# Two row tiles turned by transfer instead of on TensorE, and two gradient rows computed earlier

## The chip, the cores and the metric

The kernel runs on one core of a Trainium2 chip. A core has five engines that run side by side and wait for each other through semaphores: TensorE (PE, matrix products), VectorE (DVE), ScalarE (ACT), GpSimd (POOL) and SyncE (SP). SP's main work here is to issue transfers (DMAs), which 16 transfer engines carry out. An engine works through its instructions in the order that was fixed when the kernel was built; so does the queue of transfers that SP issues. The metric is device time in microseconds (us), lower is better.

## The reference

The reference computes one block and all its gradients. `xn` is the layer norm of the input `x` (2048 rows, 1024 columns); the output is `x + A(xn) + B(xn)`, where A is a gated long convolution and B is a gated network. Only B and its backward pass matter for this change:

```
gate = xn @ W_gate                 # 1024 -> 3584
up   = xn @ W_up
h    = relu(gate) * up
out += h @ W_down                  # 3584 -> 1024
# backward, with g the gradient of the output:
gh   = g @ W_down^T
grad_up, grad_gate = gh * relu(gate), gh * (gate > 0) * up
# and from these the gradients of W_gate, W_up, W_down and of x
```

All tensors are bf16; products are summed in f32.

## The kernel before

**Tiles and blocks.** Rows come in 16 tiles of 128, and the 3584 hidden columns in 7 blocks of 512. The first phase, `hidden`, goes over 14 blocks: 7 column blocks for row tiles 0 to 7, then the same 7 for row tiles 8 to 15. For each block and row tile it makes three products with `gemm8` (line 1088), each of 8 matmuls 128x128 by 128x512: the gate into `ps_g`, the up into `ps_u`, and the gradient row (`grad_row`) into `ps_h`. The first two read a turned tile of normalised rows (`xT[s]`, tile `xnT`: the contraction has to lie along the partitions) and the weight tiles `wg` and `wu`. The third reads a turned tile of the gradient (`gT[s]`, tile `goT`) and the turned `W_down` (`wdT`). ACT copies the gate through a ReLU into `ru` (line 1196); DVE masks the up (1203) and makes `ht` (1209), which is stored to `h_d` (1214). After a gradient row, ACT copies `ps_h` to `gh` (1331), DVE multiplies `ru` by it (1332), and `ru` is stored to `ug_d` (1337).

**Where turned tiles come from.** `goT` and `wdT` are read from DRAM by transposing transfers that SP issues (`load_T`, line 1112; `row_piece_T`, 1106). The normalised rows don't exist at the start: the layer norm makes them in the first block, chunk by chunk (`layer_norm`, a generator that is advanced by `next(ln)`; `chunk` takes three steps). DVE scales a tile (line 987), POOL stores it to `xn_d` (990), and in the first block `flip_xn` turns it: 8 PE transposes of 128x128 into a PSUM bank (line 1127, `pst_x`) and one or two copies to `xnT` (1132). For row tiles 8 to 15, in the second half, `xnT` is read back from `xn_d` by transposing transfers.

**Order in the first block** (`n == 0`, `ahead` is true). `first_rows` makes gates and ups of rows 0 to 3. Then the loop over `sp = 0, 2, 4, 6` issues: gradient rows `sp` and `sp + 1` (`grad(sp)`), and gates and ups of rows `sp + 4` and `sp + 5` (`gate_up(sp + 4)`), as long as there are any. So the order is: gradient rows 0, 1; gates and ups 4, 5; gradient rows 2, 3; gates and ups 6, 7; gradient rows 4, 5, 6, 7. Within `grad(0)` tiles 4 and 5 are turned, and within `grad(2)`, after the first matmul of row 3, tiles 6 and 7 (`flip_ahead`).

**Weights of the next block.** At the end of `gate_up(6)` the transfers for the second block are traced: `wg` (`load_gate`), `wu` (`load_up`, line 1081) and the second half of `wdT` (`load_down(2)` and `load_down(3)`). The new `wg` is put where the old one lies, so its first piece waits until gate row 7 has read that piece; so does `wu`, behind the ups. The new `wdT` has a place of its own.

**What sets an engine's order.** The instructions of this stretch have priorities by the order of the code (`pri.now()`), and a scheduler takes on each engine, by its own model of time, the first in priority that is ready. An instruction that waits for nothing, such as the transfers of `goT` and `wdT`, can so be issued ahead of older ones that wait. `tc.issue_after(ins)` keeps the instructions traced under it behind `ins`, if they are on the same engine as `ins`; it has no effect on other engines.

Of the kernel before, what the change touches and what calls it, by code (L numbers as in the profile page):

```python
# [17 lines left out]
P = 128  # L18
# [854 lines left out]
class LnMlp:  # L873
# [246 lines left out]

    def flip_xn(self, st):
        xT = self.act_tile("xnT", st)
        h = self.DT // 2 if st < 3 else self.DT
        for k0 in range(0, self.DT, h):
            pst = self.ps.tile([P, self.DT, P], BF16, name="pst_x", tag="bps")
            for kt in range(k0, k0 + h):
                self.pri.pin(self.nc.tensor.transpose(pst[:, kt, :], self.xn[st][:, kt * P:(kt + 1) * P],  # L1127
                                                      self.ident[:]), always=True)
            c = h // 2 if st == 0 and k0 == 0 else h
            for k in range(k0, k0 + h, c):  # L1130
                copy = self.nc.scalar.copy if st == 4 else self.nc.vector.tensor_copy
                self.copied = copy(out=xT[:, k * P:(k + c) * P], in_=pst[:, k:k + c, :].rearrange("p a b -> p (a b)"))  # L1132
                if st < 5:
                    self.tc.keep_in_program_order(self.copied)
        return xT
# [11 lines left out]
    def hidden(self, first, goT, load, ln, tables, Wg, Wu, Wd, g, xn_d, h_d, ug_d):  # L1147


        nc, HS, N = self.nc, self.ST // 2, 2 * self.FB  # L1150
        w, sets, spare = first, (0, 1, 2), 3
        self.g_nat, self.hs = [None] * self.ST, [None] * (self.ST // 2)
        xT, gT = [], goT
        for n in range(N):
            half, fb = divmod(n, self.FB)
            s0, cols, ahead = half * HS, slice(fb * 512, fb * 512 + 512), n == 0
            swap, last = fb == self.FB - 1, n == N - 1
            if n and fb == 0:
                xT, gT = nxT, ngT
# [8 lines left out]
            def load_gate():  # L1168
                if last:
                    self.slab_part(h_d, 0, "hs", self.hs, 4, sg)  # L1170
                else:
                    nw[0] = self.col_block(Wg, nb, "wg", sg)

            def load_up():
                if not last:
                    nw[1] = self.col_block(Wu, nb, "wu", su)

            def load_down(q):
                if last and q == 0:
                    self.slab_part(h_d, 0, "hs", self.hs, 0, spare)  # L1180
                elif not last:
                    if q == 0:
                        nw[2] = []
                    nw[2].append(self.row_piece_T(Wd, nb, "wdT", spare, q))

            def flip(k):
                while len(xT) < k:
                    while len(self.xn) <= len(xT):
                        next(ln)
                    xT.append(self.flip_xn(len(xT)))  # L1190

            def gate(s, held=False):
                ru[s] = self.e2_tile("ru")
                ps = self.ps_tile("ps_g")
                self.gemm8(ps, xT[s], wg)
                self.pri.pin(nc.scalar.activation(out=ru[s][:, 0, :], in_=ps[:], func=ACT.Relu), always=held)  # L1196

            def up(s, mid=None, after={}, put=lambda *fs: [f() for f in fs], hold=False):
                ps = self.ps_tile("ps_u")
                self.gemm8(ps, xT[s], wu, mid, after)  # L1200

                def masked():
                    return self.pri.pin(nc.vector.scalar_tensor_tensor(  # L1203
                        out=ru[s][:, 1, :], in0=ru[s][:, 0, :], scalar=0.0, in1=ps[:], op0=ALU.is_gt, op1=ALU.mult),
                        always=hold)

                def product():
                    ht = self.e1_tile("ht")
                    self.pri.pin(nc.vector.tensor_tensor(out=ht[:], in0=ru[s][:, 0, :], in1=ru[s][:, 1, :],
                                                         op=ALU.mult), always=hold)  # L1210

                    def store(r=(s0 + s) * P, cols=cols, ht=ht):
                        queue = nc.gpsimd if n == 0 and s < 4 else nc.sync
                        self.stored = queue.dma_start(out=h_d[r:r + P, cols], in_=ht[:])
                        self.pri.pin(self.stored)
                    self.defer(store)
                put(masked, product)

            def step(ns=1730):
                yield ns  # L1220
                self.tick()
# [41 lines left out]
            def gate_up(sp):  # L1263
                end = sp == HS - 2
                if ahead:
                    flip(sp + 2)
                for s in (sp, sp + 1):
                    gate(s)
                    yield from step(self.PACE[0])
                if end:  # L1270
                    load_gate()
                for s in (sp, sp + 1):
                    up(s)
                    yield from step(self.PACE[1])
                if end:
                    load_up()
                    if ahead:
                        for q in range(2, 4):
                            load_down(q)
                if swap:  # L1280
                    next_rows(sp)

            def next_rows(sp):
                for s in (sp, sp + 1):
                    if last:
                        self.g_nat[2 * sp + s - sp] = self.load_nat(g, 2 * sp + s - sp, "g_nat", s)
                    else:
                        nxT.append(self.load_T(xn_d, HS + s, "xnT", s))
# [32 lines left out]
            def flip_ahead(sp):  # L1321
                flip(min(sp + 6, HS))
                if sp == 0:
                    with self.tc.issue_after(self.copied.ins):
                        chunk()

            def grad_row(s, after={}):
                ps = self.ps_tile("ps_h")
                self.gemm8(ps, gT[s], wd, None, after)
                gh = self.e1_tile("gh")  # L1330
                self.pri.pin(nc.scalar.copy(out=gh[:], in_=ps[:]))  # L1331
                self.pri.pin(nc.vector.tensor_tensor(out=ru[s][:], in0=ru[s][:], in1=gh[:].rearrange(
                    "p (o f) -> p o f", o=1).to_broadcast([P, 2, 512]), op=ALU.mult))

                def store(r=(s0 + s) * P, cols=cols, t=ru[s]):
                    queue = nc.gpsimd if n == 0 and s < 2 else nc.sync
                    self.pri.pin(queue.dma_start(out=ug_d[r:r + P, :, cols], in_=t[:]))
                self.defer(store)
                yield 1730
                self.tick()  # L1340
# [8 lines left out]
            def grad(sp):  # L1349
                for s in (sp, sp + 1):  # L1350
                    at = 3 if sp == 0 else 0
                    yield from grad_row(s, {at: lambda: flip_ahead(sp)} if ahead and s == sp + 1 else {})
                if swap:
                    next_grads(sp)

            def chunk(steps=3):
                with self.tc.issue_after(self.ln_act.ins):
                    for _ in range(steps):
                        next(ln)
# [8 lines left out]
            for sp in range(0, HS, 2):  # L1368
                self.pri.now()
                while len(gT) < min(sp + 4, HS):  # L1370
                    gT.append(self.load_T(g, len(gT), "goT", HS + len(gT)))
                if ahead or sp < HS - 4:
                    if not ahead:
                        load_down(sp // 2)
                        yield from gate_up(sp)
                        self.hold = self.busy = False
                    yield from grad(sp)
                elif sp == HS - 4:
                    yield from last_rows(sp)
                if ahead:  # L1380
                    with self.tc.issue_after(self.stored.ins):
                        if sp in (0, 4):
                            load(6 + sp // 4)
                        if sp == 0:
                            for q in range(2):
                                load_down(q)
                if ahead and sp + 4 < HS:
                    yield from gate_up(sp + 4)
                if n == 1 and sp in (0, 2):
                    with self.tc.issue_after(self.stored.ins):  # L1390
                        load(8 + sp // 2)
                if ahead and sp == 4 or n == 1 and sp in (0, 6):
                    chunk()
                if ahead and sp == 4:
                    with self.tc.issue_after(self.ln_act.ins), self.tc.issue_after(self.ln_dve.ins):
                        tables()
# [474 lines left out]
```

## Time and profile before

| what | before |
|---|---|
| time, median of 3 runs | 1856.0 us (1855.65 to 1856.48) |
| profiled execution | 1856.27 us, of which the span from first to last instruction is 1854.5 us |
| granted TensorE clock | 1.000 of full speed |
| DVE, ACT, POOL busy, share of the span | 60%, 35%, 1% |
| chain that ended last | PE 99%, DMA 1% |
| matmul 128x512, mean duration (they overlap) | 379 ns |
| transposes of `xn` on PE (`pst_x`), 64 of them | 219 ns median duration, 7.2 to 38.1 us |
| copies `xnT` from PSUM on DVE | 11, of 0.278 to 0.692 us |
| transposing transfers `goT`, time on SP's queue | 1.259 / 1.427 / 3.837 us (least, median, most) |
| transposing transfers `wdT`, time on SP's queue | 1.246 / 1.344 / 4.083 us |

Times within the profile count from the span's first instruction. "SPq" is the queue on which SP issues transfers; the time shown there is that of issuing, and a transfer lands later. The time of a transposing transfer that stands in the timeline is therefore no time of arrival. The first block is the stretch up to about 53 us, and the whole change lies in it.

### The profile page before, as it was taken

The numbers are of one execution on the slowest core, as the hardware profiler recorded it, in microseconds if no ns is written. First come the engines' busy times: TensorE is split into PE (matmuls) and PEld (weight loads), VectorE is DVE, ScalarE is ACT, GpSimd is POOL, SyncE is SP. The second block draws the span as 40 slices with busy tenths as digits, with TensorE's granted clock in tenths as the row PEclk, the third lists the DMA queues.
The fourth block names the chain that finished last, engine by engine and source line by source line (L and its number), as shares of the span: only waits on it lengthen the run. The fifth ranks groups of instructions, "written<-read, shape, count | busy, mean of one in ns | idle before, by whom it ended". The sixth has DMA issues, their size and how long they took to land.

```text
span 1854.5 us, 32107 instructions
## 1 busy us (share of the span) xinstructions
PE 1846.5 (100%) x13061; PEld 846.8 (46%) x13061; DVE 1115.5 (60%) x1634; ACT 646.5 (35%) x1215; POOL 26.6 (1%) x63
## 2 busy tenths in 40 slices
PE   9999999999999999999999999999999999999999
PEld 4444444444444444444444444444444544444444
DVE  6656797698779769585785667721122222566652
ACT  5644544444444454544544554320000000111100
POOL 1000000000000000000000000000000000000000
PEclk9999999999999999999999999999999999999999
DMA  9897679968766857549566444379999757799963
GB/s 271 240 222 185 155 170 228 233 153 202 171 165 192 257 138 186 129 133 251 155 156 162 138 132 140 125 220 260 246 250 247 181 144 165 177 210 214 207 149 74
DMA packets 746084, 344.64 MB, mean 186 GB/s; under 512 B 575832, under 2 KB 715088, under 8 KB 745936
## 3 DMA queue, kind: packets, MB, share of 16 engines
q1 hardware_dynamic: 732944, 312.96, 70.5%
q10 hardware_dynamic: 9504, 17.04, 2.9%
q0 software_dynamic: 3488, 12.58, 1.9%
q8 instruction: 102, 1.67, 0.4%
q14 instruction: 46, 0.38, 0.1%
HBM read 143.79 MB, written 103.83 MB: 134 GB/s over the span
## 4 chain that ended last, share of the span: by engine, by line
PE 99%; DMA 1%; ACT 0%; DVE 0%; issue 0%; ACTq 0%; DVEq 0%
PE ps_x L1721 21%; PE ps_w L1424 20%; PE ps_h L1088 10%; PE ps_u L1088 10%; PE ps_g L1088 10%; PE ps_o L1589 10%; PE ps_d L1424 9%; PE ps_c L83 4%; PE ps_d L1440 2%; PE ps_w L1440 1%; DMA wu<-in_B_W_up_dram 0%; PE ps_r L1623 0%; DMA ug_d<-ru 0%; DMA ln_x<-in_A_q_dram 0%; PE pst_x L1127 0%; ACT arena L87 0%
## 5 line engine op out<-in xcount | busy, mean ns | idle before, releaser
L1424 PE MATMUL ps_w<-ugs,xn_nat 128*128 128x512 bf16 x1728 | 381.1, 379 | 0.0
L87 ACT CAST arena<-ps_c 128x512 bf16<-128x512 f32 x576 | 293.9, 610 | 84.8 <-PE ps_c L83 84.4
L1088 PEld LDWEIGHTS <-xnT 128*128 128x128 bf16 x1792 | 171.8, 98 | 209.7 <-issue 6.5
L1424 PEld LDWEIGHTS <-xn_nat 128*128 128x128 bf16 x1728 | 165.3, 98 | 201.2 <-issue 6.7
L341 DVE STREAM_TRANSPOSE arena<-arena 128x1024 f32<-128x1024 f32 x96 | 180.3, 1933 | 126.4 <-ACT arena L87 108.5
L1088 PE MATMUL ps_u<-wu,xnT 128*128 128x512 bf16 x896 | 206.0, 379 | 0.6 <-DMA wu<-in_B_W_up_dram 0.6
L1088 PE MATMUL ps_g<-wg,xnT 128*128 128x512 bf16 x896 | 205.1, 379 | 0.4 <-DVE xnT L1132 0.3
L1088 PE MATMUL ps_h<-wdT,goT 128*128 128x512 bf16 x896 | 203.8, 379 | 1.0 <-ACT ru L1196 1.0
L1721 PE MATMUL ps_x<-wgT,ggT 128*128 128x512 bf16 x896 | 198.6, 379 | 0.0
L1721 PE MATMUL ps_x<-wuT,guT 128*128 128x512 bf16 x896 | 198.6, 379 | 0.0
L1739 ACT ACTIVATE w<-xn,m 128x512 f32<-128x512 bf16 x32 | 24.3, 807 | 481.6 <-DVE m L1732 368.2
L1589 PE MATMUL ps_o<-wd,hT 128*128 128x512 bf16 (+1 forms) x896 | 187.6, 372 | 0.0
L1424 PE MATMUL ps_d<-g_nat,hs 128*128 128x512 bf16 x768 | 169.9, 379 | 0.0
L1721 PEld LDWEIGHTS <-guT 128*128 128x128 bf16 x896 | 87.7, 98 | 105.7
L1721 PEld LDWEIGHTS <-ggT 128*128 128x128 bf16 x896 | 87.7, 98 | 105.5
L1088 PEld LDWEIGHTS <-goT 128*128 128x128 bf16 x896 | 86.5, 98 | 105.1 <-issue 2.5
L1589 PEld LDWEIGHTS <-hT 128*128 128x128 bf16 x896 | 87.7, 98 | 99.9
L1331 ACT CAST gh<-ps_h 128x512 bf16<-128x512 f32 x112 | 66.3, 592 | 189.2 <-PE ps_h L1088 177.6
L1427 ACT CAST wi<-ps_w 128x512 bf16<-128x512 f32 x108 | 64.6, 598 | 189.7 <-PE ps_w L1424 155.4
L1203 DVE SCALAR_TENSOR_TENSOR ru<-ru,ps_u 128x512 bf16<-128x512 bf16 x112 | 76.3, 682 | 84.2 <-PE ps_u L1088 46.8
L1581 DVE TENSOR_TENSOR ya<-ya,xe 128x1024 bf16<-128x1024 bf16 x16 | 11.1, 692 | 177.3 <-DMA xe<-xn_d 177.3
L91 DVE TENSOR_TENSOR t<-arena 128x2048 bf16<-128x2048 bf16 x96 | 113.8, 1218 | 0.4
(146 smaller groups left out, 1402.1 us busy)
## 6 DMA issues: line engine op xcount, KB each, us to landing
ugs<-ug_d SPq DMA_DIRECT2D x112, 256.0 KB
ug_d<-ru SPq DMA_DIRECT2D x110, 256.0 KB
wg<-in_B_W_gate_dram SPq DMA_DIRECT2D x56, 256.0 KB
wu<-in_B_W_up_dram SPq DMA_DIRECT2D x56, 256.0 KB
hs<-h_d SPq DMA_DIRECT2D x56, 256.0 KB
out_dram<-wi SPq DMA_DIRECT2D x56, 256.0 KB
h_d<-ht SPq DMA_DIRECT2D x108, 128.0 KB
gt<-in_grad_out_dram SPq DMA_DIRECT2D x32, 256.0 KB
```

The costliest lines, as they stand in the source:

```text
L83: self.pri.pin(self.nc.tensor.matmul(out, lhsT=lhsT, rhs=rhs, start=start, stop=stop))
L87: self.pri.pin(self.nc.scalar.copy(out=out, in_=in_))
L91: self.pri.pin(self.nc.vector.tensor_tensor(out=out, in0=in0, in1=in1, op=op))
L341: self.pri.pin(self.nc.vector.transpose(out=df[:, c0:c0 + 32, :], in_=sf[:, c0:c0 + 32, :]))
L1088: self.pri.pin(self.nc.tensor.matmul(ps[:], lhsT=xT[:, kt * P:(kt + 1) * P], rhs=w(kt), start=(kt == 0), stop=(kt == self.DT - 1)), always ...
L1203: return self.pri.pin(nc.vector.scalar_tensor_tensor(out=ru[s][:, 1, :], in0=ru[s][:, 0, :], scalar=0.0, in1=ps[:], op0=ALU.is_gt, op1=ALU ...
L1331: self.pri.pin(nc.scalar.copy(out=gh[:], in_=ps[:]))
L1424: self.pri.pin(self.nc.tensor.matmul(ps[:], lhsT=lhsT(st), rhs=rhs(st), start=(st == 0), stop=(st == self.ST - 1)))
L1427: self.pri.pin(self.nc.scalar.copy(out=out, in_=ps[:]))
L1440: self.pri.pin(self.nc.tensor.matmul(ps[i][:], lhsT=lhsT(i, st), rhs=rhs(i, st), start=(st == 0), stop=(st == self.ST - 1)))
L1589: nc.tensor.matmul(ps, lhsT=hT[:, kt, :], rhs=self.wd[:, kt, oc], start=(kt == 0), stop=(kt == self.FT - 1))
L1721: nc.tensor.matmul(ps, lhsT=T[:, kt, :], rhs=W[:, kt, oc], start=(i == 0), stop=(i == n - 1))
```

## The change

Three edits. First, `flip_xn` turns tiles 6 and 7 (`st > 5`) by a transposing transfer on SP that reads the normalised tile in on-chip memory (SBUF) and writes `xnT` there, in place of eight PE transposes and a DVE copy for each; the last such transfer is kept as `self.turned`. Second, in the first block two groups of transfers on SP are kept behind `self.turned`: the second half of the next `wdT`, and `goT` 6 and 7. (For `goT` 4 and 5 the edge goes to `self.copied`, a DVE instruction, and has no effect on SP.) Third, `grad(4)` is traced right after `grad(2)`, ahead of `gate_up(6)`; the order of the products in the first block becomes: gradient rows 2, 3, 4, 5; gates and ups 6, 7; gradient rows 6, 7.

```diff
     def flip_xn(self, st):
         xT = self.act_tile("xnT", st)
+        if st > 5:
+            self.turned = self.nc.sync.dma_start_transpose(out=xT[:].rearrange("p (a b) -> p a b", b=P),
+                                                           in_=self.xn[st])
+            return xT
         h = self.DT // 2 if st < 3 else self.DT
...
                 if end:
                     load_up()
                     if ahead:
-                        for q in range(2, 4):
-                            load_down(q)
+                        with self.tc.issue_after(self.turned.ins):
+                            for q in range(2, 4):
+                                load_down(q)
...
             for sp in range(0, HS, 2):
                 self.pri.now()
                 while len(gT) < min(sp + 4, HS):
-                    gT.append(self.load_T(g, len(gT), "goT", HS + len(gT)))
+                    with self.tc.issue_after(self.turned.ins if sp == 4 else self.copied.ins):
+                        gT.append(self.load_T(g, len(gT), "goT", HS + len(gT)))
...
-                    yield from grad(sp)
+                    if not ahead or sp != 4:
+                        yield from grad(sp)
+                    if ahead and sp == 2:
+                        yield from grad(4)
```

## The prediction

> **What bounds the kernel.** I read the page's busy times first, then what TensorE (PE) waits for after 12 us, then the timelines of PE and of SP's queue in the first 60 us, and last the busy share of the transfer engines in that stretch.
>
> ```profile
> PE 1846.5 (100%) x13061; PEld 846.8 (46%) x13061; DVE 1115.5 (60%) x1634; ACT 646.5 (35%) x1215; POOL 26.6 (1%) x63
> ```
>
> PE is busy for 1846.5 of 1854.5 us. What shortens PE's own work shortens the kernel; any new wait of PE lengthens it, for there is almost no wait in which to hide one:
>
> ```profile
> PE ps_h L1088 <- ACT ru L1196: 1.0, 1, 1.0
> PE ps_u L1088 <- DMA wu<-in_B_W_up_dram: 0.6, 1, 0.6
> PE ps_g L1088 <- DVE xnT L1132: 0.3, 1, 0.3
> ```
>
> (In total, times, longest.) From 12 us on PE waits three times, for 1.9 us together, the third of them at the very start. Now PE around the change (start, length, what, count):
>
> ```profile
> 35.74 1.67 PE L1088 MATMUL ps_h<-wdT,goT 128*128 128x512 bf16 x7
> 37.26 1.06 PE L1127 MATMUL pst_x<-ident,ln_x 128*128 128x128 bf16 x16
> 38.15 1.67 PE L1088 MATMUL ps_h<-wdT,goT 128*128 128x512 bf16 x7
> 39.66 3.62 PE L1088 MATMUL ps_g<-wg,xnT 128*128 128x512 bf16 x16
> 43.11 3.62 PE L1088 MATMUL ps_u<-wu,xnT 128*128 128x512 bf16 x16
> 46.57 7.07 PE L1088 MATMUL ps_h<-wdT,goT 128*128 128x512 bf16 x32
> 53.47 3.62 PE L1088 MATMUL ps_g<-wg,xnT 128*128 128x512 bf16 x16
> ```
>
> The 16 transposes of tiles 6 and 7 sit inside gradient row 3; then come gates and ups of rows 6 and 7 (39.66, 43.11), gradient rows 4 to 7 in one run (46.57), and at 53.47 the second block, which needs new weights wg and, from 56.93, wu. The queue that fetches them:
>
> ```profile
> 33.19 3.00 SPq L1112 DMA_TRANSPOSE goT<-in_grad_out_dram  x2
> 36.24 3.02 SPq L1106 DMA_TRANSPOSE wdT<-in_B_W_down_dram  x2
> 39.30 4.02 SPq L1112 DMA_TRANSPOSE goT<-in_grad_out_dram  x2
> 43.44 0.99 SPq L1214 DMA_DIRECT2D h_d<-ht  x2
> 44.52 1.31 SPq L1337 DMA_DIRECT2D ug_d<-ru  x2
> 45.93 2.17 SPq L1081 DMA_DIRECT2D wg<-in_B_W_gate_dram  x4
> ...
> 53.03 1.25 SPq L1337 DMA_DIRECT2D ug_d<-ru  x2
> ```
>
> SP issues without a pause from 33.19 to 51.39, and the transfer engines are full (stretch, length, busy time of each engine; the last three figures are the granted clock, the transfer engines' busy share and GB/s):
>
> ```profile
> 36.20:43.30 7.10, 7.10 (x46) 3.71 (x45) 3.62 (x7) 1.77 (x3) 1.02 (x2) 1.00 1.26 231
> 43.30:48.10 4.80, 4.80 (x24) 2.18 (x23) 2.22 (x4) 0.60 (x1) 0.00 (x0) 1.00 0.92 260
> 48.10:51.40 3.30, 3.30 (x17) 1.53 (x16) 1.25 (x2) 1.77 (x3) 0.00 (x0) 1.00 0.94 273
> ```
>
> Shares of 0.92 to 1.26 mean that whatever is added lands later. When each transfer lands is in the trace's semaphore records (each transfer raises its semaphore in 16 steps; the last one counts); PE's need is the start of the matmul that reads the piece:
>
> ```
> transfer   SP issue      landed   PE needs it   margin
> goT 4, 5   33.19-36.20   37.43, 38.25
> wdT 2, 3   36.24-39.26   41.23, 43.68
> goT 6, 7   39.30-43.33   44.56, 45.48
> ug_d 2, 3  44.52-45.83   47.14, 47.94
> wg 0..3    45.93-48.10   49.51 50.55 52.23 52.97   53.47 53.90 54.34 54.77   3.96 3.35 2.11 1.80
> wu 0..3    48.19-51.39   53.68 54.73 55.45 56.50   56.93 57.36 57.79 58.22   3.25 2.63 2.34 1.72
> ```
>
> The smallest margin, 1.72 us (wu's last piece), carries the forecast.
>
> **Part by part.**
>
> *16 PE transposes go.* The first starts at 37.26, the matmul behind them at 38.15: **0.89 us** of PE time saved (55.6 ns each). Tiles 6 and 7 alone change. Weighed against a rule: the Trainium skill (TensorE: Matmul & The Clock Gate, "Part 4: PE-mode transpose") gives about 275 ns for such a transpose inside a kernel, by which 16 would be 4.4 us, an estimate from that page. Here they follow each other at 55.6 ns in a full pipeline, so the row decides.
>
> *Two DVE copies go* (1.28 us at 38.47). DVE is idle for 3.9 us at 41 to 45; PE waits for no later DVE result here: nothing. If that cover were gone, at most 1.28.
>
> *Gradient rows 4 and 5 move ahead of gates 6 and 7.* The same 16 matmuls, 3.45 us, at another place: nothing for PE. They need goT 4 and 5 at 38.77 and 40.50 instead of 46.57 and 48.30; landed at 37.43 and 38.25, so nothing, with 1.3 us to spare. Behind the late PE instructions gates 6 and 7 start at 39.66 − 0.89 + 3.45 = 42.22 and at 43.95.
>
> *Two SP transposes are added.* They wait for the normalised tiles; DVE scales them at 35.35 to 36.22 and SP is free at 36.2, so SP hardly stands still. In the queue they take the places of wdT 2 and 3, which landed at 41.23 and 43.68; needed 42.22 and 43.95. Just in time, 1.0 and 0.3 us to spare, a little less if the store of h row 4, ready at 35.4, is issued ahead. No row of this trace is a transpose out of on-chip memory. The nearest are the wdT and goT transposes, of the same 256 KB: from below, 0.9 us between landings when nothing disturbs them (43.68, 44.56, 45.48); from above, (45.48 − 38.25)/4 = 1.81, other traffic included. SP itself spends 1.36 to 1.66 us on most of them. I take 1.2 each, between the transfer's 0.9 and SP's 1.5, since both limit here: **2.4 us for the two, 1.8 to 3.6**. A rule that would lower it: the Trainium skill (DMA: Bandwidth & Descriptors, "Why small descriptors are slow (HBM only)" and "Where 436 GB/s comes from") says that on-chip copies don't suffer from small pieces and that 435 GB/s bounds them, transposes included; that makes 0.6 us each, an estimate from that page, and the end 1.2 us earlier than by my value. No run here shows it.
>
> *wdT 2, 3 and goT 6, 7 are queued behind those two.* goT 6 and 7 land some 2.4 us later, at 47 and 48; their rows now start at 42.22 + 6.91 = 49.13 and 50.86. wdT is wanted in the second block at 60.4. Nothing by themselves; but all four still stand ahead of wg, and so the whole queue moves back by the 2.4.
>
> *The stores of rows 4 and 5 (ug_d) overtake the weights.* This is no line of the diff. Rows 4 and 5 now end at 42.22 and their products are ready some 1.5 us after; wg can't be fetched before gate 7 has read the old piece (43.95 + 0.43). So these stores, at 53.03 before, come ahead of wg. ug_d 2 and 3 landed 0.80 us apart: **1.6 us** for two. If they stay behind, nothing.
>
> *The gate of the old weights.* wg comes free at 44.4 to 45.7 instead of 41.8 to 43.1; since SP reaches wg only after 45.93 anyway, this adds nothing to the queue.
>
> *Sum.* wg and wu land 2.4 + 1.6 = 4.0 us later (3.4 to 5.2), and PE wants them 0.89 earlier. wu's last piece: 56.50 + 4.0 = 60.5 against 57.33: PE loses 3.2 in several waits at the second block's start and has gained 0.89. Net: 4.0 − 1.72 = **+2.3 us** (+1.7 to +3.5). Later work has no wait to absorb that. The profiled execution took 1856.27 us (span 1854.5 and 1.8 around it), 0.27 over the median of 1856.0: it becomes 1858.6, the median **1858.3**.
>
> **Rivals.**
>
> 1. *All hidden* (1855.1). The new transposes fill a hole: between 42.1 and 43.7 transfers lay still here (wdT 3 and goT 6 land 0.9 after that), and if the stores stay behind wg and the hole takes most of the two transposes, the shift stays under 1.72 − 0.89 = 0.8 us. Then only −0.89 is left. For it: the hole is in the record. Against: SP needs 1.36 us for each issue in any case, and the stores are ready too early. In between, stores behind and transposes at 1.2, lies 2.4 − 1.72 = +0.7, 1856.7.
>
> 2. *Slower outright* (1861.9). Transposes out of on-chip memory run at the worst pace of this stretch, 2.98 us (38.25 to 41.23): 6.0 + 1.6 − 1.72 = +5.9. Gate 6 would then wait too, but that wait lies ahead of the same late weights and is not added. It is over 0.2% from 1.9 + a little us per transpose on: (3.7 + 1.72 − 1.6)/2 = 1.9. For it: no row shows such a transpose, and these already swing between 0.9 and 3. Against: packet size and count would be alike.
>
> 3. *A larger gain*: the 16 transposes cost their shown duration, 219 ns each, 3.5 us, with nothing late: 1852.5; and the rule above would give 1851.6. The pitch of 55.6 ns speaks against it.
>
> 4. *The change doesn't do what it says*: the transposes are issued behind other stores, and PE waits at 42.22 for about as long as it saved: 1856.0 to 1857.
>
> **Numbers.** Forecast (+1.7 to +3.5): 0.46. Stores behind (about +0.7): 0.12. All hidden: 0.20. Slower outright (over +3.5): 0.15. Larger gain: 0.02. Not as said: 0.05. Two in ten left out, most of them in the slow tail and the large gain: 1855.0 to 1860.4. A measurement of this kernel tells about 0.2% (3.7 us) from no change. Below 1852.3 lies only rival 3 in its larger form, 0.02; above 1859.7 rival 2 and a little of the forecast's upper end, 0.15; the rest, 0.83, is within.
>
> **What would show it.** PE's timeline: no pst_x at 37, row 3 in one run, rows 4 and 5 at 38.8, gate 6 at 42.2 without a wait. SP's timeline: goT 4, 5, two xnT, wdT 2, 3, goT 6, 7, then stores of four rows ahead of wg. PE's waits: DMA wg and DMA wu at the second block's start, about 3 us in all; with none of these, rival 1 holds. Gates 6 and 7 waiting for xnT by over 1 us, or two xnT landing more than 1.9 us apart, is rival 2. The forecast is wrong if wg is issued before the stores of rows 4 and 5, or if the queue reaches wg less than 2.5 us later than at 45.93.

## The result and the profile after

The kernel after takes **1863.04 us** in the median of 7 runs (1861.35 to 1870.74), the kernel before 1856.07 us in 7 runs beside it (1855.65 to 1856.48): ratio 1.0041 (over all runs; the two medians alone give 1.0038), 95% interval 1.0031 to 1.0051. The forecast was 1858.3 us (1855.0 to 1860.4). The direction was right, and so was the first part of the mechanism, weights that come late at the second block's start; what follows from these waits was missing, and the size was not right. The profiled execution took 1863.04 us with a span of 1861.3 us, 6.8 more than before's.

Busy times of the page, and what PE waits for from 12 us on (in total, times, longest):

```profile
PE 1835.6 (99%) x12833; PEld 846.5 (45%) x13045; DVE 1115.1 (60%) x1632; ACT 644.6 (35%) x1213; POOL 26.6 (1%) x63
```
```profile
PE ps_g L1088 <- DMA wg<-in_B_W_gate_dram: 2.6, 3, 1.1
...
PE ps_h L1088 <- ACT ru L1200: 2.4, 1, 2.4
...
PE ps_h L1088 <- DMA goT<-in_grad_out_dram: 1.0, 2, 0.7
```

PE's busy time is no measure here, since 212 matmul records are missing (12833 against 13045 weight loads). The waits tell more: those for `wg` are the forecast ones; `goT` is new, and the one for ACT's `ru` has grown from 1.0 to 2.4 us. PE around the change:

```profile
35.58 7.07 PE L1088 MATMUL ps_h<-wdT,goT 128*128 128x512 bf16 x31
42.49 3.62 PE L1088 MATMUL ps_g<-wg,xnT 128*128 128x512 bf16 x16
45.94 3.62 PE L1088 MATMUL ps_u<-wu,xnT 128*128 128x512 bf16 x16
49.95 3.79 PE L1088 MATMUL ps_h<-wdT,goT 128*128 128x512 bf16 x15 [0.39 <-DMA goT<-in_grad_out_dram]
54.62 1.30 PE L1088 MATMUL ps_g<-wg,xnT 128*128 128x512 bf16 x4 [0.89 <-DMA wg<-in_B_W_gate_dram]
56.49 0.59 PE L1088 MATMUL ps_g<-wg,xnT 128*128 128x512 bf16 x2 [0.57 <-DMA wg<-in_B_W_gate_dram]
58.20 4.00 PE L1088 MATMUL ps_g<-wg,xnT 128*128 128x512 bf16 x10 [1.12 <-DMA wg<-in_B_W_gate_dram]
```

Gradient rows 2 to 5 run as one group, without the transposes, and gate 6 starts at 42.49 without a wait (forecast 42.22). Then each piece of `wg` lets PE do two matmuls and wait again. The queue on SP that brings them:

```profile
36.53 0.52 SPq L1218 DMA_DIRECT2D h_d<-ht  x1
37.15 4.02 SPq L1124 DMA_TRANSPOSE xnT<-ln_x  x2
41.26 0.53 SPq L1218 DMA_DIRECT2D h_d<-ht  x1
41.84 1.23 SPq L1106 DMA_TRANSPOSE wdT<-in_B_W_down_dram  x1
43.17 0.68 SPq L1342 DMA_DIRECT2D ug_d<-ru  x1
43.90 2.38 SPq L1106 DMA_TRANSPOSE wdT<-in_B_W_down_dram  x1
46.32 1.30 SPq L1112 DMA_TRANSPOSE goT<-in_grad_out_dram  x1
47.73 0.56 SPq L1342 DMA_DIRECT2D ug_d<-ru  x1
48.33 1.38 SPq L1112 DMA_TRANSPOSE goT<-in_grad_out_dram  x1
49.81 1.21 SPq L1342 DMA_DIRECT2D ug_d<-ru  x2
51.11 2.21 SPq L1081 DMA_DIRECT2D wg<-in_B_W_gate_dram  x4
```

`wg` is issued at 51.11 instead of 45.93: 5.18 later. It landed at 54.58, 55.29, 56.45 and 58.16, which is 4.2 to 5.2 later. Last, stretches of 1 us (length, busy time of PE, PEld, DVE, ACT and POOL, then the granted clock, the transfer engines' share and GB/s):

```profile
57.00:58.00 1.00, 0.08 (x1) 0.00 (x0) 0.97 (x7) 0.00 (x0) 0.18 (x2) 1.00 1.01 322
58.00:59.00 1.00, 0.80 (x3) 0.32 (x3) 1.00 (x3) 0.00 (x0) 0.00 (x0) 0.66 1.03 384
59.00:60.00 1.00, 1.00 (x4) 0.36 (x3) 0.48 (x1) 0.82 (x2) 0.00 (x0) 0.50 1.10 412
60.00:61.00 1.00, 1.00 (x3) 0.29 (x2) 0.00 (x0) 1.00 (x1) 0.00 (x0) 0.50 1.03 379
61.00:62.00 1.00, 1.00 (x4) 0.39 (x3) 0.55 (x2) 0.41 (x2) 0.15 (x1) 0.63 1.07 396
62.00:63.00 1.00, 1.00 (x6) 0.48 (x5) 0.25 (x1) 0.76 (x2) 0.00 (x0) 1.00 1.05 389
```

The granted clock falls to half at 58.32 for 3.41 us, and PE's weight loads follow each other at 0.43 us instead of 0.216, though now its data is there.

Every execution has its mean granted clock on record. One fall of 3.41 us lowers the mean of 1861 us by 0.0009, so 0.999 tells of one such fall and 0.998 of two. (The clock falls also behind PE's last matmul; in the profiled spans that lasts at most 1.3 us, too little for the third digit.) Two of the seven executions have 1.000 and took 1861.35 and 1862.31 us; three have 0.999 and took 1862.71 to 1863.57; two have 0.998 and took 1863.92 and 1870.74. So the clock is only a part of the loss: without a fall 5 to 6 us are left.

**Where the 6.8 us lie.** I matched PE's weight loads of both traces one by one and took the lag of after (a start in after less that of the same load in before):

```
at 50 us (gain -0.89, lag from before row 2 +0.27, goT 6 +0.55)     -0.06
waits for goT 7 and the four pieces of wg, 50 to 58.2 us            +3.49
clock at half, 58.3 to 61.7 us                                      +1.69
132 to 144 us                                                       +0.68
278 us (a wait for wu of before is gone)                            -0.78
353 to 359 us (ACT's ru, behind a store of ug_d)                    +1.36
end                                                                 +0.43
sum                                                                 +6.81
```

The wait at 353 to 359 us on ACT's side:

```profile
358.87 0.60 ACT L1200 ACTIVATE ru<-ps_g 128x512 bf16<-128x512 f32 x1 [5.42 <-DMA ug_d<-ru]
```

### The profile page after: what moved, and what is told of

The parts are those of the page before. It is cut to its first block, busy times and chain, and to the rows that moved or that the text cites. A ratio compares the mean times of both kernels' runs of the same rounds, so it can differ in the third digit from the quotient of the medians.

```text
span 1861.3 us, 31864 instructions
## 1 busy us (share of the span) xinstructions
PE 1835.6 (99%) x12833; PEld 846.5 (45%) x13045; DVE 1115.1 (60%) x1632; ACT 644.6 (35%) x1213; POOL 26.6 (1%) x63
## 4 chain that ended last, share of the span: by engine, by line
PE 94%; DMA 2%; SPq 1%; issue 1%; DVE 0%; ACT 0%; ACTq 0%; DVEq 0%
PE ps_x L1730 21%; PE ps_w L1433 20%; PE ps_o L1598 10%; PE ps_h L1088 10%; PE ps_u L1088 9%; PE ps_g L1088 9%; PE ps_d L1433 9%; PE ps_c L83 4%; PE ps_d L1449 1%; SPq L1106 1%; PE ps_w L1449 1%; DMA goT<-in_grad_out_dram 1%; DMA wg<-in_B_W_gate_dram 1%; DMA wu<-in_B_W_up_dram 0%; DMA ugs<-ug_d 0%
## 5 line engine op out<-in xcount | busy, mean ns | idle before, releaser
L1433 PE MATMUL ps_w<-ugs,xn_nat 128*128 128x512 bf16 x1675 | 375.7, 379 | 4.4 <-issue 2.4
```

The source lines that it names most:

```text
L1433: self.pri.pin(self.nc.tensor.matmul(ps[:], lhsT=lhsT(st), rhs=rhs(st), start=(st == 0), stop=(st == self.ST - 1)))
```

## The experiments

The theory after this result: the bytes that now stand ahead of `wg` make it late, and the idle time that follows trips the clock. The rivals were the order of the products, the transposes' kind of memory, the place in SP's queue, and a cost of the late part of the kernel. Times are medians, with the range and number of runs; ratios are to the kernel before on the same chip, where its median was 1856.0 to 1857.1 us, and are worked out over all runs, so they are not quite the quotients of the medians. Each edit is to the kernel that is named.

**e1: the order alone** (before, with the third edit of the change; PE still turns all tiles).

```diff
-                    yield from grad(sp)
+                    if not ahead or sp != 4:
+                        yield from grad(sp)
+                    if ahead and sp == 2:
+                        yield from grad(4)
```


> Only the order of the products is changed; tiles 6 and 7 are turned on PE as before. Theory Q (the weights wg and wu land late because two transposing transfers, 4.0 us of SP's time, and the stores of gradient rows 4 and 5, 1.2 us, come ahead of them; the waits then halve the clock for 3.4 us): only the 1.2 of the stores is left, wg lands 1.2 to 1.6 us later than before, which is under its margin of 1.8 us, so PE waits 0 to 0.3 us and the time is before + 0 to 0.5 (1856.0 to 1856.6). Rival O (the order alone is at fault, since the old weights come free 2.6 us later): waits of 2 us and more at the second block's start, 1858 or more.

1856.8 us (1855.5 to 1860.4, 11), ratio 1.0006 (0.9997 to 1.0014). The stores go as forecast, four together and ahead of `wg` (SP's queue):

```profile
44.88 2.68 SPq L1337 DMA_DIRECT2D ug_d<-ru  x4
47.65 2.27 SPq L1081 DMA_DIRECT2D wg<-in_B_W_gate_dram  x4
```

`wg`'s last piece lands at 54.25, 1.28 later than before, which the margin of 1.80 takes: no wait. The order alone costs nothing that these runs can tell (the interval would still hold 2.6 us).

**e2: the transfers alone** (after without the third edit: `grad(4)` stays where it was).

```diff
-                    if not ahead or sp != 4:
-                        yield from grad(sp)
-                    if ahead and sp == 2:
-                        yield from grad(4)
+                    yield from grad(sp)
```

> Only the two transposing transfers; gradient rows 4 and 5 stay behind gates and ups 6 and 7. Gate 6 is then due at 38.8 us and tile 6 lands at about 42.2: PE waits 3.4 us there. Theory Q: net 3.4 - 0.9 = +2.5 if the clock holds and about +4.2 if a wait of 3.4 us halves it for 3.4 us; wg is 4 us late but so is PE, so no wait of more than 0.5 us at the second block's start (1858.5 to 1860.3). Rival O: this version without the new order is near before, 1855 to 1857.

1869.02 us (1865.44 to 1872.71, 5), ratio 1.0070 (1.0058 to 1.0083): slower than the whole change, and far above the 1858.5 to 1860.3 expected, which counted one long wait and at most one fall of the clock.

```profile
PE ps_g L1088 <- DMA xnT<-ln_x: 4.1, 1, 4.1
PE ps_h L1088 <- DMA goT<-in_grad_out_dram: 3.6, 2, 3.5
```

Gate 6 is now wanted 3.5 us earlier and waits 4.1 us for its tile; the scheduler also put `goT` 7 behind `wu`, so that PE waits again. The clock falls to half for 3.41 us with each of the two waits. So the third edit, taken together with the transfers, saves more than it costs by bringing two stores ahead of `wg`: it is what buys the transposed tiles their time.

**e3: the clock by itself** (after, with 14 matmuls that nobody reads at the end of the first block).

```diff
             self.hold = self.busy
+            if ahead:
+                ps = self.ps_tile("ps_fill")
+                for _ in range(14):
+                    self.pri.pin(nc.tensor.matmul(ps[:], lhsT=xT[0][:, 0:P], rhs=gT[0][:, 0:512], start=True,
+                                                  stop=True), always=True)
```


> The changed kernel with 14 matmuls (3.0 us) added at the end of the first block, whose result nobody reads; they fill the time in which PE waits for wg. Theory Q with the clock: the clock stays at 1.00 in the second block, and although PE has 3.0 us more work the time falls by 1.3 to 1.7 us, to 1861.3 to 1861.8. Rival C (the clock's drop at 58.3 us has nothing to do with the waits): the clock drops all the same and the time stays at 1863 or rises.

1861.30 us (1860.18 to 1863.06, 7), ratio 1.0028 (1.0016 to 1.0039): 1.74 us *faster* than after (by the medians of two sets of runs, beside which before took 1856.01 and 1856.07), with 14 matmuls (3.0 us at 0.216) more work. They fill the time in which PE waited for `wg`. The granted clock is 1.000 in all seven executions; in stretches of 2 us around the place:

```profile
56.00:58.00 2.00, 2.00 (x11) 0.88 (x9) 1.43 (x11) 0.88 (x1) 1.99 (x5) 1.00 1.04 309
58.00:60.00 2.00, 2.00 (x11) 0.90 (x10) 1.97 (x9) 0.61 (x2) 0.69 (x3) 1.00 1.02 358
```

So 1.7 us of the loss is the clock, and it answers to PE standing idle, not to what it waits for.

**e4 and e5: one group each out from ahead of `wg`.** e4 is after with the stores of gradient rows 4 and 5 behind `wu`, e5 is after with `wdT` 2 and 3 behind `wu` (`self.loaded`, new in both, is the last transfer of the weights).

```diff
e4
-                self.defer(store)
+                if n == 0 and s in (4, 5):
+                    self.kept.append(store)
+                else:
+                    self.defer(store)
...
+                if ahead and sp == 2:
+                    with self.tc.issue_after(self.loaded.ins):
+                        for f in self.kept:
+                            f()
e5
-                        with self.tc.issue_after(self.turned.ins):
+                        with self.tc.issue_after(self.loaded.ins):
                             for q in range(2, 4):
                                 load_down(q)
```


> The changed kernel, but the two stores of gradient rows 4 and 5 are issued on SP behind wu. Theory Q: wg lands 1.2 us earlier than in the changed kernel, the waits for it fall from 3.3 to about 2.1 us, net 1.2 us less, 1861.8; if the shorter waits spare the clock, another 1.7 less, 1860.1. If the stores' place does not matter (transfers limited elsewhere): 1863.0.

> The changed kernel, but the second half of the next wdT (two transposing transfers, 1.7 us of SP each) is issued on SP behind wu instead of ahead of wg. Theory Q: SP reaches wg about 3.5 us earlier than in the changed kernel, that is 1.5 us later than before, within the margin of 1.8 us; no wait for wg, none for goT 6, the clock stays, and what is left is PE's saving: before - 0.9 to before (1855.1 to 1856.0). Rival W (wdT itself is then late: it lands at 58 to 60 us and row 0 of the second block reads its third piece at 60.3): PE waits up to 2 us there, 1856 to 1858.

e5: 1858.88 us (1856.34 to 1863.02, 11), ratio 1.0013 (1.0004 to 1.0022); 1.1 us of waits for `wg` and 1.2 for `wu` are left where none was expected, and the clock holds in the profiled execution; `wdT` makes PE wait in neither e5 nor e6, so the rival there is out. e4: 1863.84 us (1859.91 to 1865.18, 5), ratio 1.0036 (1.0023 to 1.0049), no gain in the median. In its profiled execution the second block's start did what was expected (0.7 us for `wg`, 1.1 for `wu`, full clock), but the place at 353 us, far from the change, got worse:

```profile
353.22 1.90 PE L1089 MATMUL ps_u<-wu,xnT 128*128 128x512 bf16 x8
358.65 3.57 PE L1089 MATMUL ps_h<-wdT,goT 128*128 128x512 bf16 x8 [3.53 <-ACT ru L1202]
```

PE waits 3.5 us for a `ru` of ACT, and the clock is at half for 6.83 us (the eight matmuls of 358.65 take 3.57 us instead of 1.9): about 5.4 us more than before at this place alone. The clock divides the five executions of e4: two at 1.000 took 1859.91 and 1859.96 us, which is what was expected with the clock spared; three at 0.999 or 0.998 took 1863.84 to 1865.18.

**e6: both together** (e4 and e5).

> As the run before, and the stores of gradient rows 4 and 5 also behind wu and wdT. Theory Q: wg lands about 0.3 us later than before; no waits at the second block's start, before - 0.9 to before - 0.5 (1855.1 to 1855.5). Rival W: the same late wdT as in the run before, and the stores, now later still, may hold up ru in the second block: 1856 to 1858.

1858.8 us (1856.26 to 1861.43, 11), ratio 1.0012 (1.0003 to 1.0020). PE's waits in its profiled execution of 1856.26 us:

```profile
PE ps_h L1089 <- ACT ru L1202: 0.9, 1, 0.9
PE ps_h L1089 <- DVE ru L1209: 0.7, 1, 0.7
```

No wait at the second block's start is left, the clock holds, and at 50 us PE is 1.24 us ahead of before; at 144 us this lead is gone (0.27 behind). The easing is worth 4.2 us of the 7.0, but the median stays 2.4 above before's 1856.4. Here, too, the clock divides the executions: five at 1.000 took 1856.26 to 1857.95 us, six at 0.999 took 1858.80 to 1861.43.

**e7 and e8: what two more transposes cost, and whether their source matters.** Both are before, plus two transposed transfers of 256 KB into memory that nobody reads; PE still turns all tiles. In e7 the source is the normalised tile on chip, in e8 the gradient in DRAM.

```diff
e7
+        if st > 5:
+            t = self.ln_x[3][:, st - 4, :]
+            self.nc.sync.dma_start_transpose(out=t.rearrange("p (a b) -> p a b", b=P), in_=self.xn[st])
e8
+        if st > 5:
+            t = self.ln_x[3][:, st - 4, :]
+            self.nc.sync.dma_start_transpose(out=t.rearrange("p (a b) -> p a b", b=P), in_=self.g_rows[st * P:(st + 1) * P, :])
...
+        self.g_rows = g
```


> The kernel before (PE transposes, old order), with two transposing transfers of the normalised tiles 6 and 7 added on SP ahead of wg, into memory that nobody reads. Theory Q: SP reaches wg 3.3 to 4 us later; PE's need is unchanged, margins 1.72 to 1.8, so waits of 1.5 to 2.3 us at the second block's start, net the same (1857.5 to 1858.3), up to 1860 if the clock drops. Rival S (a transfer that reads on-chip memory is dearer than one that reads DRAM): over 1 us worse than the run after this one.

> The same with the two added transfers reading the gradient's rows in DRAM. Theory Q: a transposing transfer costs SP about 1.7 us whichever memory it reads, so the same delay of wg and the same time as the run before this one within 1 us (1857.5 to 1858.3). Rival S: 1 us or more faster than that run.

e7: 1858.61 us (1856.25 to 1859.81, 10), ratio 1.0011 (1.0002 to 1.0020). e8: 1857.76 us (1856.13 to 1860.03, 10), ratio 1.0007 (0.9997 to 1.0016). The two intervals overlap almost wholly. On SP's queue the pair took 2.62 us in e7 and 1.31 + 1.51 in e8:

```profile
46.17 2.62 SPq L1125 DMA_TRANSPOSE ln_x<-ln_x  x2
```

`wg` was issued 4.98 us later than in before in e7 and 2.08 later in e8, but there the queue itself had come to `goT` 4 1.77 us later and 1.25 earlier. From the issue of `goT` 4 to that of `wg` it is 15.94 and 16.06 us, against 12.73 in before: 3.2 and 3.3 us for the pair. So no difference between on-chip and DRAM source is to be seen on the queue, and nothing speaks against pricing them by the DRAM rows of before. (The scheduler placed the two differently: behind `goT` 6 and 7 in e7, ahead of `wdT` 2 and 3 in e8. So this is no clean comparison of what they cost PE.)

**e9 to e11: another queue.** The second block's weights are issued on POOL's queue: `wg` and `wu` in e9 (on after) and e10 (on before), `wg` alone in e11 (on after).

```diff
-            self.pri.pin(self.nc.sync.dma_start(out=t[:], in_=W[...
+            queue = self.nc.gpsimd if fb == 1 and name in ('wg', 'wu') and not self.pri.strict else self.nc.sync
+            self.pri.pin(queue.dma_start(out=t[:], in_=W[...
```


> The changed kernel, but wg and wu for the second block are issued by POOL on its own queue instead of SP. Theory Q (they are late because they stand behind transposes and stores in SP's queue): wg is issued as soon as gate 7 frees it, from about 44.8 us, lands by 52, no waits for wg or wu, clock at 1.00; before - 0.9 to before + 0.3 (1855.1 to 1856.3). Rival E (the transfer engines are full, whichever queue issues): the bytes ahead of PE's need stay the same, so goT 6 and 7, which share the engines with wg now, land later instead, PE waits 1 to 3 us for them, 1857 to 1861.

> The kernel before with wg and wu for the second block issued by POOL. Nothing waited for them there, so Theory Q and rival E both expect no change, 1855.5 to 1856.5; it is the control for the run before. Under rival E goT 6 and 7 may land later, but their need at 50.0 and 51.8 us leaves 5 us.

> The changed kernel with wg alone on POOL's queue, wu on SP. Theory Q: no wait for wg; wu is issued at 51.1 instead of 53.4, lands 2 us earlier, no wait either; same as the run with both, 1855.1 to 1856.3. Rival E: as there, 1857 to 1861.

e9: 1871.14 us (1862.11 to 1875.19, 6), ratio 1.0076 (1.0058 to 1.0094), the slowest of all. e11: 1864.18 us (1861.55 to 1865.63, 5), 1.0039 (1.0027 to 1.0051). e10: 1855.94 us (1855.31 to 1857.44, 11), 0.9997 (0.9989 to 1.0006). PE in e9:

```profile
46.13 3.62 PE L1089 MATMUL ps_u<-wu,xnT 128*128 128x512 bf16 x16
54.67 3.59 PE L1089 MATMUL ps_h<-wdT,goT 128*128 128x512 bf16 x8 [4.92 <-DMA goT<-in_grad_out_dram]
60.28 2.31 PE L1089 MATMUL ps_h<-wdT,goT 128*128 128x512 bf16 x5 [2.02 <-DMA goT<-in_grad_out_dram]
63.67 3.76 PE L1089 MATMUL ps_g<-wg,xnT 128*128 128x512 bf16 x16
```

Now `wg` is on time and `goT` 6 and 7 are late: the same transfers stand ahead of them on SP's queue as in after, and still they land at 54.62 and 60.24 us instead of 49.90 and 51.79. So the weights on the second queue take from the same transfer engines, and `goT`, which is needed earlier, is what PE waits for. It is the bytes ahead of the need that cost, not the place on one queue; that part of the theory falls. With the room that before has, the same move (e10) does nothing.

**e12 and e13: two more microseconds of room.** e12 is e6 with the 512 KB load of layer-norm rows 6 and the work on them moved later, out from ahead of `wg`; e13 is e12 with tiles 6 and 7 turned on PE again.

```diff
e12
-                        if sp in (0, 4):
-                            load(6 + sp // 4)
+                        if sp == 4:
+                            load(6)
+                            load(7)
...
-                if ahead and sp == 4 or n == 1 and sp in (0, 6):
+                if n == 1 and sp in (0, 2, 6):
                     chunk()
```


> The kernel after with both easings of e6 (the stores of gradient rows 4 and 5 and the transfers of wdT 2 and 3 issued behind wu) and a third: the 512 KB load of the layer norm's rows 6 is issued later in the first block and the work on them is moved one block on, which takes about 2 us more of transfers out from ahead of wg. Theory (the whole loss is bytes that are due ahead of PE's need, against queue positions that scatter by 1 to 2 us): with another 2 us free nothing at block 2's start can come late, and PE's saving of 0.89 us is left: 1855.1 to 1855.8, and a narrower scatter than e6's 1856.3 to 1861.4. Rival (the rest of the loss in e6, about 2 us in the median, is elsewhere, such as at the late wait near 353 us): 1858 to 1859 as in e6.

> The kernel e12 with normalised row tiles 6 and 7 turned on PE again: the same easing of the queue without the two transfers. Theory: the time of the kernel before, 1855.8 to 1856.4, since before never waits there, so that e12 less e13 is PE's saving, -0.5 to -0.9 us. Rival: if the two transfers cost something else than their place in the queue, e13 is faster than e12 by 1 us or more.

e13: 1856.29 us (1855.69 to 1858.23, 11), ratio 1.0000 (0.9992 to 1.0009): the easing by itself neither gains nor costs. e12: 1858.28 us (1854.80 to 1859.92, 11), ratio 1.0009 (1.0000 to 1.0018), where 1855.1 to 1855.8 was expected. The theory that only the weights' lateness costs is too narrow. The profiled execution of e12 shows a wait that e6's did not:

```profile
PE ps_g L1089 <- DMA xnT<-ln_x: 1.1, 1, 1.1
PE ps_h L1089 <- ACT ru L1202: 0.4, 1, 0.4
PE ps_h L1089 <- DMA goT<-in_grad_out_dram: 0.3, 1, 0.3
```

Gate 6 waits for its transposed tile. It landed at 43.85 and was wanted at 42.8. In the other profiled kernels with this order it had arrived 0.31 us (after), 0.07 (e3), 0.19 (e4), 0.15 (e5), 0.41 (e6), 0.04 (e9) and 0.81 (e11) ahead of gate 6, where positions in the queue differ by 1 to 2 us from execution to execution (in the four profiled executions of e12's kernel tile 6 landed between 42.30 and 44.18).

**e14: one tile less** (e12, with tile 6 on PE and only tile 7 by transfer).

```diff
-        if st > 5:
+        if st > 6:
```

> The kernel e12 with tile 6 turned on PE again and only tile 7 by a transposed transfer. Theory (what is left in e12 is the transposed tiles themselves coming late: tile 6 landed only 0.04 to 0.8 us ahead of gate 6 in seven profiled kernels of this study and 1.1 us behind it in e12, with queue positions that scatter by 1 to 2 us): tile 7 alone lands one transpose earlier, about 42.3 in e12's positions, and is read 1.73 us later, so that some 2 to 3 us of margin are left; half of PE's saving stays, -0.45: 1855.6 to 1856.3, against e13 1856.3. Rival (the rest of e12's loss is elsewhere, at goT 6 and 7 or near 353 us): 1857.5 to 1858.5, as in e12.

1858.0 us (1855.62 to 1859.98, 11) against 1857.09 beside it (1855.45 to 1858.13, 15): ratio 1.0006 (0.9997 to 1.0015). In the profiled execution no wait for `xnT` is left. The median, though, is nearer to the rival's; the interval holds no change as well as 2.8 us. Inconclusive.

**e15 to e17: the kernel e12 profiled three times more**, to see where single executions lose.

> The kernel e12 profiled once more. An execution near its median (1858.3, 2 us over the one profiled first) is wanted, to see in which place it loses them: theory A, gate 6 or 7 waits for its transposed tile by 1 us or more; theory B, a wait of row 6 or 7 for goT; theory C, the late place near 353 us, where a PE wait for ACT of over 1.4 us stands against 0.4 in e12's first profile.

> As e15: a further execution of the kernel e12, with the same three places: A, a wait for the transposed tile of 1 us or more; B, a wait for goT 6 or 7; C, a PE wait for ACT near 353 us of over 1.4 us.

> As e15 and e16: a third execution of the kernel e12, with the same three places. If all three lose at one place, that place is the rest of the loss; if each loses at another, the rest has no single cause.

They took 1855.43, 1858.78 and 1855.98 us, and PE waited 0.2, 0.9 and 0.8 us for the transposed tile; with e12's first profile, 0.75 us in the mean. That gives back most of the 0.89 that PE saves. The longest, e16:

```profile
PE ps_h L1089 <- DVE ru L1209: 1.4, 1, 1.4
PE ps_g L1089 <- DMA xnT<-ln_x: 0.9, 1, 0.9
PE ps_h L1089 <- ACT ru L1202: 0.9, 1, 0.9
PE ps_h L1089 <- DMA goT<-in_grad_out_dram: 0.4, 1, 0.4
```

It loses in four places, the largest at about 133 us. The rest of e12's loss has no single cause in these four.

But all four ran at a granted clock of 1.000, and the timed executions of e12 did not. Six of its eleven have 1.000 and took 1854.80 to 1858.28 us, 1856.38 in the median, as much as before's 1856.39; the other five have 0.999 and took 1858.62 to 1859.92. In e13 one of eleven has 0.999, in before beside them none of 21. So most of what e12 loses in the median comes with a fall of the clock in nearly half of its executions. Which wait trips it is not seen, since no profiled one has the fall.

## Why the prediction was wrong

The forecast was a loss of 2.3 us; the profiled execution lost 6.81. Of the 4.5 us between, 1.1 lie at the second block's start, where the lag was 3.43. Another 1.7 are the half clock behind the last wait, and 1.7 more come later (0.68 − 0.78 + 1.36 + 0.43). For these two the sum had nothing: it closes with the last late piece, as if the lag would then stay what it is. This is the step that failed most.

*What bounds the kernel: right.* PE had no wait in which to hide one, and everything that came late was paid for at once.

*16 PE transposes go, 0.89 us: right.* Row 3 runs through in one group; gate 6 starts 2.83 us later than in before, which is the 3.45 of rows 4 and 5, less 0.89, with the lag of 0.27 from earlier. e6 is 1.24 us ahead of before at 50 us with nothing late, of which 0.35 are the start. Rival 3, and the Trainium skill's 275 ns for each transpose with it (TensorE: Matmul & The Clock Gate, "Part 4: PE-mode transpose"), are out by the same 0.89.

*Rows 4 and 5 ahead: right.* e1 costs nothing that can be told; `goT` 4 and 5 make PE wait nowhere in after. With 1.3 us to spare this was near: row 5 waited for its `goT` for 0.21 us in e5 and 0.69 in e9, row 4 for 1.05 in e11.

*Stores of rows 4 and 5 overtake the weights, 1.6 us: right,* and 1.28 by the landings of e1.

***Two SP transposes, "2.4 us for the two": too small; this is the term that failed first.*** `wg` was issued 5.18 us later. Of this 0.55 is a later start (SP issued `goT` 4 at 33.74 instead of 33.19), and the stretch from there to `wg` is 4.64 longer. By the queue's own rows six transposes took 10.3 us of SP (4.02 + 1.23 + 2.38 + 1.30 + 1.38) where four took 7.04, so 3.3 for the two, as in e7 and e8; the other 1.3 are the stores. Reckoned by landings (5.19 less the 1.28 of e1) it is 3.9. So the pair cost 3.3 to 3.9: near or just past the upper bound of 1.8 to 3.6, and 0.9 to 1.5 above the 2.4 of the sum. I had taken the middle of two prices at which a transpose runs when little disturbs it, in a stretch whose engines were full, where the rows of before already held 1.8 each. With the measured shift the same sum gives 5.2 − 1.80 = +3.4 at the second block's start, and +3.43 was the lag there (before the clock fell). The two are not dear by their source: e7 and e8 agree.

***"PE loses 3.2 in several waits": the waits were priced, what follows them was not.*** The sum ends with the last late piece. In the trace, PE then ran at half clock for 3.41 us, +1.69 us; e3 takes it away and gets 1.74 back. The Trainium skill (TensorE: Matmul & The Clock Gate, "Part 1: The HAM clock gate") says that the clock halves after an idle window of about 3.4 us, in windows that run freely. The trace agrees on the length (3.413 us, or twice or three times that), but not on the idle window: no single wait here was longer than 1.12 us, and PE still did some 1.1 us of work in the 3.41 us ahead of the fall. The rule bore on the forecast, which had named 3 us of waits in one place, and was not weighed there. How the waits trip the clock is worked out in the last section.

*"Later work has no wait to absorb that": true, and yet the loss grew.* At 353 us ACT's `ru` waits for a store of `ug_d`, and PE for ACT: 2.4 us in after against 1.0. In e4 it was 3.5, with the half clock beside it; in e6 0.9, in e15 0.3. All that is shown is that it varies from kernel to kernel and from execution to execution, by more than the whole margin argued about; why it tended to be longer with the transfers is open. So are 0.68 us at 132 to 144 us, where e6's profiled execution lost 1.5.

*wdT and goT behind the two, "nothing by themselves": half right.* `wdT` was not waited for. `goT` 6, forecast to land at 47 with 2 us to spare, landed at 49.90 when it was wanted at 49.4: PE waited.

*Gates 6 and 7 without a wait: right in after, by 0.31 us.* Such a margin is not one: e2, e12 and its three further profiled executions show the wait.

*The rivals.* "All hidden" and "doesn't do what it says" are out by the views above. "Slower outright" gave a time close to the result (1861.9) by a price of 2.98 us for each transpose, which isn't what happened: they cost 1.6 to 2.0 each, the two `xnT` landed 0.90 us apart (42.18 and 43.08) and gate 6 did not wait, so by its own signs this rival is out. That its time came close is luck; the clock and the late place made up the rest.

*What is left open.* With everything behind the transposed tiles eased (e12), 2.0 us in the median stand between turning them by transfer and on PE (e13). Up to 1 us of this is the wait for the tile itself, 0.75 in four profiled executions, which cancels PE's gain. The rest goes with the granted clock: e12 at 1.000 takes 1856.38 in the median, as long as before, and at 0.999 it takes 2.8 us more, of which a fall of 3.41 us by itself is 1.7. What trips the clock in these executions isn't settled, and e14 did not settle it. No version here beats the kernel before: the fastest medians beside it, e10 and e13, are the same within 0.1%.

## What to carry to other kernels

Where the transfer engines are full, a transfer that relieves a busy engine is paid for by whatever is due next: count the bytes ahead of each need, price them by the rows of that very stretch, and set the shift against the smallest margin *and* against the scatter of positions (1 to 2 us here). When the sum foresees some 3 us of waits close together, add what the granted clock does after them (here 1.7 us for a fall of 3.41), and look at the granted clock of every execution before you look for further causes. Moving the late transfer to a second queue only changes who is late, if both queues use the same engines.

## What the runs showed of the hardware

The clock's fall comes in steps: 3.41 us (after, e2 twice, e11, e9 twice, and e13 once, at 7.63 us), 6.83 (e4), 10.24 (e9). It doesn't take one long wait: in after, PE did about 1.1 us of work (by the matmuls' pitch of 0.216 us) in the 3.41 us that end with the fall at 58.32, and in e9, where a wait of 2.04 us was enough at 145.86, some 1.2 us. The length of a wait alone doesn't tell: one of 2.4 us (after, at 357 us) and one of 2.2 (e5) passed at full clock. With windows that run freely, as the Trainium skill has them (in the section cited above), a wait can be shared by two of them.

The traces bear this out. Every stretch between two changes of the clock, at full or at half, is a whole number of 3.413 us (51.20 us in after is 15 of them, 351.57 in e4 is 103), so each trace has a fixed grid of windows. Counted by weight loads at their pitch, from 12 us on, eight windows at full clock ended with a fall, and PE had worked 0 to 1.21 of the 3.41 us in them: 1.14 in after, 0 and 0.28 in e2, 0.73 in e4, 0, 1.21 and 0.99 in e9, 0.51 in e11. In every other window at full clock, up to PE's last matmul, it had worked 1.50 us or more, in all 19 traces. The wait of 2.4 us in after passed because it lies in two windows, with 1.71 and 2.59 us of work; the one in e5 left 1.63. So what counts is the work within one window. Where the windows lie differs from execution to execution: in the four profiled executions of e12's kernel the first one at full clock begins at 5.55, 6.63, 6.22 and 6.48 us. That the same waits therefore trip the clock in one execution and pass in the next is likely, but no pair of traces of one kernel shows it.

The time that a transposed transfer of 256 KB holds SP differs widely: 1.24 to 1.28 us in e7, 1.58 and 2.34 for the two of after, and 3.71 for `goT` 7 in e9, where a second queue was at work.
